# Attention features and a feed-forward on one core: block 0 turned by TensorE, two banks for small results, w1 scaled by halves, filled gaps, a new order

## The chip, the cores and the metric

The kernel runs on one core of a Trainium2 chip. TensorE (PE in the profile) multiplies matrices and writes to PSUM, eight banks of 512 fp32 columns; VectorE (DVE) and ScalarE (ACT) compute on tensors and read PSUM; GpSimd (POOL) computes on tensors in SBUF; SyncE (SP) issues the DMAs. Each engine works through its own instructions in order. The metric is device time of one execution in microseconds (us); 935.58 us is the median of three runs of the kernel before.

## The reference

Eight batches of eight heads, 576 positions, head size 64, 128 random features, then a feed-forward over the 4608 rows of 512:

```python
def phi(x):
    proj = einsum('bhsd,md->bhsm', x, omega)
    h = proj - sum(x * x, axis=-1, keepdims=True) / 2.0
    return exp(h - max(h, axis=-1, keepdims=True)) / sqrt(m)
q_p, k_p = phi(q * scale), phi(k * scale)
kv = einsum('bhsm,bhsd->bhmd', k_p, v)
z = sum(k_p, axis=2)
x = einsum('bhsm,bhmd->bhsd', q_p, kv) / (einsum('bhsm,bhm->bhs', q_p, z)[..., None] + 1e-06)
h = x.transpose(0, 2, 1, 3).reshape(4608, 512) @ w_in
out = maximum(0.01 * h, h) @ w_out
```

The weights `w_in` (512 x 2048) and `w_out` (2048 x 512) arrive as 64-bit floats, which the kernel converts on the chip.

## The kernel before

Most fp32 products are made of three fp16 products: each operand is scaled by a power of two and split into a high and a low half (`high` and `low_`, L358 and L373; the lines L369 and L375 of the profile are these two helpers).

The work is written as a list of operations with their engines, inputs, outputs and assumed durations. `Plan.order` (L128) puts them in one order before anything runs: it keeps a clock for each engine, places each operation at the earliest moment that its inputs, its buffer and its engine allow, and prefers those of lower `prio`. Products of the feed-forward are *fillers* with the last priority (`work = 1e6 + j`): they take PE whenever nothing else is ready. `PACE`, `LATER`, `NUDGE` and `SLACK` shift priorities and times. The result is a fixed order for each engine.

In order of the data:

- `omega` (L427) loads the feature matrix and scales and splits it.
- `key_batch(b)` (L786) makes `kv` of one batch. Batches 0 and 1 (`WHOLE = 2`) and query block 0 use class `Whole` (L665): the columns of k or q are loaded (L677), squared on ACT (L678), projected in full fp32 on PE (L699) into a bank pair `pj` or `pj0`; DVE takes the maximum (L706) and subtracts it (L708), ACT takes the exponential (L710). The sums over keys are L817. Later batches use class `Unit` (L560): fp16 halves, turned by a transposing DMA (L607), projected at L620.
- `values(b)` (L726) loads v (L739), finds its scale (L747 and `power_of_two`, L403) and, for batches 0 and 1, scales v in place (`high` at L762). `power_of_two` sends one column through PE into columns 384 to 511 of the bank `mi` (L409), then five small DVE operations follow.
- `query_block(j)` (L865) makes 512 rows of x. Block 0's features are turned by PE (L887) in fp32; the products with kv (L917) go to a bank `mi`, columns 0 to 259; DVE inverts and multiplies (L927 to L930) into `xp`. Then `parted` (L854) splits the rows into halves in a buffer `xn` and turns them by a transposing DMA (L862) into `xt`, whose columns are the tokens. There is one `xn` as long as `v1` lives.
- `Weight` (L457): eight 1 MB pieces of each matrix are loaded into four buffers `big` (L478, L480); ACT copies the high words (L493), DVE joins the low bits (L495, L498), PE sums magnitudes by column (L506, into a `ffn` bank `wsums` that is held until both matrices are through), the sign is put back by ACT and POOL (L511, L513) or DVE (L516). After all eight pieces `scale` (L519) finds one power of two for the matrix and `split` (L533) writes the halves (L540 or `high` and `low_`).
- `feed_forward(j)` (L1038): nine blocks of 512 rows. Blocks 0 and 1 make the first layer at L1059 (16 x 12 products of 512 columns), later blocks by a seven-product scheme at L1113; L1295 is the second layer, and L1220 that of the last two blocks. ACT applies the leaky maximum (L1068), and halves are split by ACT and POOL or DVE.

PSUM's eight banks: `pj` and `pj0` two each, three `ffn` and one `mi`; when the class `Whole` is through, the banks of `pj0` become two more for the feed-forward, called `late`.

Of the kernel before, what the change touches and what calls it, by code (L numbers as in the profile page):

```python
# [31 lines left out]
SPLIT_DVE = {"w1": [0, 1, 2, 4, 5, 7], "w2": [0, 1, 2, 3, 4, 5]}  # L32
Z_POOL = {"k": 6, "q": 7}
PACE = {"k": 17.0506, "q": 9.805, "w1": 0, "w1s": 2.5972, "w2": 15.4207, "w2s": 15.0}

WHOLE = 2
FIRST_FAST = 2
TAIL = 7
ROWS_LATE = 4
TAIL_ON = {"A11": ["DVE"], "A22": ["DVE"], "S1": ["DVE"], "S3": ["DVE"], "S2": ["POOL"], "A12": ["DVE"], "S4": ["DVE"], "T1": ["POOL"], "T2": ["DVE"], "T3": ["DVE"], "T4": ["DVE"]}  # L40
# [3 lines left out]
SLACK = {"PE": 0.5, "t": 0.5608, "qp": 0.5, "ph": 0.5, "mx": 0.5, "w": 0.25, "chain": 0.0804}  # L44
NUDGE = {"k00": -7.29, "w24": 1.48, "q61": -17.43, "k10": 0.44, "k51": 15.04, "q00": -3.82, "k53": 5.68, "w20": 3.7, "w2s6": 16.56, "k12": -4.82, "w1s0": 20.35, "q41": 14.5, "w1s4": -32.18, "w2s5": 11.73, "q72": -10.0, "q03": -2.3, "w1s7": 13.37, "w2s7": 35.19, "k61": -6.36, "w13": -2.71, "w2s3": -4.27, "q10": 5.76, "s1": -0.42, "k50": -35.27, "q70": 36.43, "q02": 2.72, "q40": 2.15, "k42": 7.0, "w25": 5.84, "q63": -12.37, "w27": 3.08, "k11": 0.9, "w26": 10.91, "w2s2": -8.29}
DMA = {"turn": 1.0, "land": 1.9}
SLOWER = {"ACT": 1.0, "DVE": 1.041, "POOL": 0.95, "PE": 1.0, "SP": 1.0}
EXP_ACT = {"k": [], "q": []}
XN_DVE = 0
SUMS_DVE = [2]  # L50
LATER = {"w1": -37.7982, "w2": 35.2434, "k": -22.3577, "q": -876.3298, "t": 0.05, "f": 0.0319, "s": -0.0535}
# [4 lines left out]
NUM_DOWN = 2.0 ** -12  # L56
OUT_UP = 2.0 ** 17 * 2.0 ** (-14 * 3)
# [5 lines left out]
PJ32 = 0.55  # L63

# [12 lines left out]
class Plan:  # L77
# [3 lines left out]
    HOP = {"PE": 0.25, "ACT": 0.08, "DVE": 0.08, "POOL": 0.10}  # L81
# [3 lines left out]
    def __init__(self, places):  # L85
        self.places, self.ops, self.over = places, [], {}
        self.wrote, self.read, self.kinds = {}, {}, {}
        self.now, self.nth, self.group = (None, 0.0), 0, None
# [10 lines left out]
    def op(self, ways, r=(), w=(), prio=0.0, slack=0.0, moved=0):  # L99
# [3 lines left out]
        o = Op()  # L103
        o.ways, o.prio, o.slack, o.moved = {e: way for e, *way in ways}, prio, slack, moved
# [23 lines left out]
    def order(self):  # L128
        free = dict.fromkeys(("PE", "ACT", "DVE", "POOL", "SP"), 0.0)
# [15 lines left out]
        for o in reversed(self.ops):  # L145
# [22 lines left out]
        def placed_at(o):  # L168
            t = o.ready
# [10 lines left out]
        while len(done) < len(self.ops):  # L180
# [86 lines left out]
def performer_ffn(ctx: ExitStack, tc, qT, kT, qn, kn, vn, omT, eye, w_in, w_out, out):  # L267
# [30 lines left out]
    banks = {"pj": (1, 1024), "pj0": (1, 1024), "ffn": (3, 512), "mi": (1, 512)}  # L298
# [88 lines left out]
    little, used_up = one("little", [P, 128]), [0]  # L387
# [39 lines left out]
    def omega():  # L427
        mx = small(1)
        op("SP", 0.45, lambda: nc.sync.dma_start(out=om32(), in_=omT), w=[(whole, "om")], moved=131072, prio=-0.9)
        op("SP", 0.45, lambda: nc.sync.dma_start(out=ident, in_=eye), w=["ident"], moved=65536, prio=-0.9)  # L430
# [23 lines left out]
        op("DVE", 1.3, split, r=[(whole, "om"), key], w=["om", "om_c"], prio=0.005)  # L454
# [943 lines left out]
```

## Time and profile before

| | us |
|---|---|
| median of three runs (931.43 to 936.42) | 935.58 |
| the profiled execution | 934.21 |
| its span, first to last instruction | 932.4 |
| PE busy in it | 886.1 |
| DVE busy | 751.1 |
| ACT busy | 608.9 |
| POOL busy | 326.6 |
| mean granted clock of PE | 0.979 of full |

Busy time of PE is not useful time alone: at a lower granted clock the same products are busy for longer. A wait in the tables is put down to the instruction that came last. The idle time of an engine matters only where that engine is on the way to the end.

### The profile page before, as it was taken

The numbers are of one execution on the slowest core, as the hardware profiler recorded it, in microseconds if no ns is written. First come the engines' busy times: TensorE is split into PE (matmuls) and PEld (weight loads), VectorE is DVE, ScalarE is ACT, GpSimd is POOL, SyncE is SP. The second block draws the span as 40 slices with busy tenths as digits, with TensorE's granted clock in tenths as the row PEclk, the third lists the DMA queues.
The fourth block names the chain that finished last, engine by engine and source line by source line (L and its number), as shares of the span: only waits on it lengthen the run. The fifth ranks groups of instructions, "written<-read, shape, count | busy, mean of one in ns | idle before, by whom it ended". The sixth has DMA issues, their size and how long they took to land.

```text
span 932.4 us, 20377 instructions
## 1 busy us (share of the span) xinstructions
PE 886.1 (95%) x8102; PEld 636.3 (68%) x8102; DVE 751.1 (81%) x1384; ACT 608.9 (65%) x905; POOL 326.6 (35%) x290
## 2 busy tenths in 40 slices
PE   4796999999999799999999999999999999999998
PEld 3784466555554686578658955786579657888887
DVE  7889888888889698888778987977988788993861
ACT  4777796557765687479756874796568555753741
POOL 2243446657765344117212531162115222210010
PEclk8698899999999999999999999999999999999999
DMA  9779234967479998689789997888598876633401
GB/s 365 288 206 298 62 58 104 239 169 152 108 151 278 278 261 195 174 219 257 171 184 230 247 223 183 210 235 186 111 234 219 199 158 164 177 75 94 134 1 46
DMA packets 279103, 171.17 MB, mean 184 GB/s; under 512 B 195296, under 2 KB 242144, under 8 KB 277984
## 3 DMA queue, kind: packets, MB, share of 16 engines
q1 hardware_dynamic: 279008, 169.87, 72.2%
q8 instruction: 63, 1.03, 0.5%
q14 instruction: 32, 0.26, 0.1%
HBM read 105.87 MB, written 16.78 MB: 132 GB/s over the span
## 4 chain that ended last, share of the span: by engine, by line
PE 79%; DVE 11%; DMA 5%; issue 1%; ACT 1%; SPq 1%; DVEq 0%; ACTq 0%
PE ffn L1295 15%; PE ffn L1113 15%; PE late L1295 11%; PE late L1113 10%; PE ffn L1059 5%; PE pj L620 5%; PE ffn L1220 5%; PE late L1220 3%; PE pj L699 2%; PE mi L817 2%; DMA qp<-ph 1%; DMA t<-z 1%; DMA xt<-xn 1%; DVE wt L498 1%; PE mi L910 1%
## 5 line engine op out<-in xcount | busy, mean ns | idle before, releaser
L1113 PEld LDWEIGHTS <-w 128*128 128x128 f16 x2352 | 227.4, 98 | 36.8 <-issue 6.8
L375 POOL TENSOR_TENSOR big<-row,big 128x512 f16<-128x512 f32 x116 | 150.2, 1306 | 258.9 <-ACT big L369 249.4
L1295 PEld LDWEIGHTS <-big 128*128 128x128 f16 x1344 | 127.2, 98 | 136.4
L1295 PE MATMUL ffn<-wt,big 128*128 128x512 f16 x816 | 190.2, 379 | 0.0
L1113 PE MATMUL ffn<-xt,w 128*128 128x256 f16 x1044 | 139.5, 273 | 3.3 <-DMA xt<-xn 3.3
L1295 PE MATMUL late<-wt,big 128*128 128x512 f16 x528 | 124.1, 379 | 0.0
L651 ACT ACTIVATE p<-p,little 128x1024 f32<-128x1024 f32 x68 | 70.1, 1030 | 55.5 <-DVE p L648 55.4
L628 DVE TENSOR_REDUCE st<-pj 128x8 f32<-128x1024 f32 x68 | 73.1, 1074 | 27.8 <-PE pj L620 27.4
L1113 PE MATMUL late<-xt,w 128*128 128x256 f16 x660 | 92.8, 273 | 0.0
L1059 PE MATMUL ffn<-xt,w 128*128 128x512 f16 x312 | 73.9, 388 | 8.5 <-DMA xt<-xn 8.2
L369 ACT ACTIVATE big<-row 128x512 f16<-128x512 f32 x128 | 77.2, 622 | 2.9 <-DVE row L1085 2.4
L648 DVE SCALAR_TENSOR_TENSOR p<-pj,sc,st 128x1024 f32<-128x1024 f32 x68 | 77.0, 1133 | 0.7
L375 DVE TENSOR_TENSOR ph<-p,ph 128x1024 f16<-128x1024 f32 x56 | 72.7, 1297 | 4.9 <-ACT ph L369 4.7
L580 ACT ACTIVATE z<-nat 128x512 f32<-128x512 f32 (+1 forms) x56 | 36.3, 649 | 57.6 <-DMA t<-z 46.8
L1059 PEld LDWEIGHTS <-w 128*128 128x128 f16 x384 | 37.0, 99 | 51.0 <-issue 12.3
L620 PE MATMUL pj<-om,t 128*128 128x128 f16 x944 | 63.8, 219 | 3.0 <-DMA t<-z 2.4
L620 PEld LDWEIGHTS <-t 128*128 128x128 f16 x944 | 57.5, 98 | 13.2 <-DMA t<-z 3.7
L1113 PE MATMUL ffn<-w,w 128*128 128x256 f16 x360 | 58.9, 273 | 1.7 <-ACT z L1240 1.7
L369 ACT ACTIVATE ph<-p 128x1024 f16<-128x1024 f32 x56 | 58.8, 1050 | 0.7
L375 POOL TENSOR_TENSOR v<-xp,v 128x768 f16<-128x768 f32 (+1 forms) x15 | 26.2, 1745 | 89.0 <-ACT v L369 88.9
L582 DVE TENSOR_REDUCE sq<-z 128x8 f32<-128x512 f32 (+1 forms) x56 | 39.5, 706 | 18.2 <-ACT z L580 18.1
L1136 ACT ACTIVATE row<-row 128x512 f32<-128x512 f32 x71 | 43.8, 624 | 11.3 <-DVE row L1129 11.1
(236 smaller groups left out, 1809.8 us busy)
## 6 DMA issues: line engine op xcount, KB each, us to landing
w<-w1d SPq DMA_DIRECT2D x196, 256.0 KB, 3.3
v<-vn SPq DMA_DIRECT2D x28, 650.0 KB, 4.7
big<-w_in SPq DMA_DIRECT2D x8, 1024.0 KB, 10.2
big<-w_out SPq DMA_DIRECT2D x8, 1024.0 KB, 5.7
nat<-qn SPq DMA_DIRECT2D x32, 256.0 KB, 3.9
out<-row SPq DMA_DIRECT2D x32, 256.0 KB, 2.6
w1d<-wt SPq DMA_DIRECT2D x16, 256.0 KB, 3.3
nat<-kn SPq DMA_DIRECT2D x12, 320.0 KB, 3.5
```

Source lines behind the costliest of these rows:

```text
L369: ("ACT", act(n, int(pointer)), lambda: nc.scalar.activation(dst(), src(), AF.Copy, scale=1.0 if scale is None else value()), False),
L375: return ways([(e, c, lambda g=g: g.tensor_tensor(dst(), a(), b(), op=ALU.subtract), True) for e, c, g in (("POOL", pool_(n), nc.gpsimd), ...
L582: op("DVE", dve(n), lambda: nc.vector.tensor_reduce(at(self.sq)[:, :2 * nt], square().rearrange("p (g d) -> p g d", d=D), axis=AX.X, op=AL ...
L620: nc.tensor.matmul(at(pj)[:, 512 * h + c * M:512 * h + (c + 1) * M], at(self.t)[:, 2 * (c0 + c) + h, :], om[:, w, :], start=(w == 0), stop ...
L628: op("DVE", dve(n * M), lambda: nc.vector.tensor_reduce(row(0), pv(), axis=AX.X, op=ALU.max), r=[pj], w=[st], prio=prio)
L648: op("DVE", dve(n * M), lambda: nc.vector.scalar_tensor_tensor(p(), pv(), down(), row(2).rearrange("p (g o) -> p g o", o=1).broadcast_to([ ...
L651: op("ACT", act(n * M, 1), lambda: nc.scalar.activation(flat(p()), flat(p()), AF.Exp, bias=shift), w=[p32], r=["ones"], prio=prio)
L1059: nc.tensor.matmul(at(ph), wk[wp][:, c:c + P], xt[:, 512 * xp:512 * xp + 512], start=(i == 0), stop=(i == 3 * KT - 1))
L1113: nc.tensor.matmul(pair(bank)[:, f], wt[:, k, wp, f * P:f * P + P], operand(xname, k, xp), start=(first and f == k == i == 0), stop=(k == ...
L1136: op("ACT", act(512), lambda: nc.scalar.activation(at(g), at(src), AF.Prelu, scale=H_DOWN * (TAIL_DOWN if tail else 1.0), alpha=0.01), r=[ ...
L1220: nc.tensor.matmul(pair(bank)[:, t], g()[:, gp, f, t * P:t * P + P], operand(wname, 2 * q + f, wp), start=(first and q == t == f == i == 0 ...
L1295: nc.tensor.matmul(at(po), g_(q)[:, s, gp, t * P:(t + 1) * P], wf[wp], start=(q == s == 0 and gp == wp), stop=(q == s == 3 and gp == 1))
```

## The change

- `TURNED = 1`: block 0's rows are turned by PE transposes into an `ffn` bank, and the halves are made from there by ACT and DVE (`turned_parts`); `parted` with its DMA is not used for it.
- `FFN_MI = [2, 2]`: two fixed `ffn` banks instead of three, two `mi` banks instead of one. The weights' column sums lie in unused columns of `mi` 0.
- w1 gets one scale for pieces 0 to 3 and one for 4 to 7; the first half can be split when four pieces are converted. w2's scale takes both into account. w2's sums add pairs of columns.
- `HEAT`: where the planned order leaves PE a gap of over 0.3 us ahead of the first filler, products that nobody reads (240 columns, into `mi` 1) are put in.
- Batches 0 and 1: v is not scaled; its column of ones is divided instead, and the scale goes into the eviction of kv. The exponentials of `Whole` lose their shift.
- `LOW_ACT`: for one piece of w1 and three of w2 ACT shifts the low word, and one DVE operation joins instead of two. `EDGE_ACT`: one edge's exponential is taken straight from PSUM by ACT. `SQ_POOL`: two squares by POOL.
- `Whole` has buffers of its own kinds, four `raw` and three `sqz`, that lie over `nat`, `t`, `xn`, `z` and `p32`; batch 1's operations are listed ahead of query block 1's.
- The planner's figures (`HOP`, `LESS`, `SLOWER`, `SLACK`, `PACE`, `LATER`, `NUDGE`, issue costs) change, and it now models the clock of PE. A second, backward pass exists but is not run (`PASSES = 0`). `EXP_ACT`, `Z_POOL`, `SPLIT_DVE` and `TAIL_ON` move some later operations between engines.

```diff
-SPLIT_DVE = {"w1": [0, 1, 2, 4, 5, 7], "w2": [0, 1, 2, 3, 4, 5]}
-Z_POOL = {"k": 6, "q": 7}
+SPLIT_DVE = {"w1": [0, 1, 2, 4, 5, 7], "w2": [0, 1, 2, 3, 4, 5, 6]}
+Z_POOL = {"k": 6, "q": 6}
+TURNED = 1
+HEAT = True
+PASSES = 0
+EDGE_ACT = ['k02']
+SQ_POOL = ['k02', 'k13']
+LOW_ACT = {"w1": [3], "w2": [1, 4, 5]}
+FFN_MI = [2, 2]
...
-SLOWER = {"ACT": 1.0, "DVE": 1.041, "POOL": 0.95, "PE": 1.0, "SP": 1.0}
-EXP_ACT = {"k": [], "q": []}
+SLOWER = {"ACT": 1.0223, "DVE": 1.0399, "POOL": 0.95, "PE": 1.0, "SP": 1.0}
+EXP_ACT = {"k": [], "q": [1]}
...
-    HOP = {"PE": 0.25, "ACT": 0.08, "DVE": 0.08, "POOL": 0.10}
+    HOP = {"PE": 0.25, "ACT": 0.13, "DVE": 0.12, "POOL": 0.13}
+    LESS = {"PE": 0.0, "ACT": 0.08, "DVE": 0.08, "POOL": 0.08, "SP": 0.0}
...
+                if HEAT and not o.filler and not begun and t - s > 0.3:
+                    x = Op()
+                    n = int((t - s - 0.1) / (0.2 if cold else 0.1))
...
+                    x.run, x.prio, x.filler, x.heat = (lambda n=n: self.warm[1](n)), 1e7, True, True
...
+                begun = begun or o.filler
...
-    banks = {"pj": (1, 1024), "pj0": (1, 1024), "ffn": (3, 512), "mi": (1, 512)}
+    banks = {"pj": (1, 1024), "pj0": (1, 1024), "ffn": (FFN_MI[0], 512), "mi": (FFN_MI[1], 512)}
...
+    for k, hosts in (("raw", (("nat", 0), ("nat", 1), ("t", 0), ("xn", 0))), ("sqz", (("z", 0), ("z", 1), ("p32", 0)))):
+        for host in hosts:
+            over[host] = [(k, len(tiles[k]))]
...
+        def heat(n):
+            for _ in range(n):
+                nc.tensor.matmul(tiles["mi"][1][:, 4 * E:4 * E + 240], om[:, 0, :],
+                                 om.rearrange("p a b -> p (a b)")[:, :240], start=True, stop=True)
+        plan.warm = done, heat
...
-            self.sums, self.col0 = wsums, 64 * (name == "w2")
+            first = 4 * E + 64 * (name == "w2")
+            self.sums = tiles["mi"][0][:, first:first + (32 if name == "w2" else 64)]
...
+            if i in LOW_ACT[self.name]:
+                op("ACT", act(1150), lambda: nc.scalar.activation(shifted(), low(), AF.Copy, scale=LOW_DOWN, bias=LOW_LESS),
+                   r=[b], w=[tmp], prio=prio)
+                op("DVE", stt(1024), lambda: nc.vector.scalar_tensor_tensor(shifted(), bits(), 3, shifted(),
+                   op0=ALU.logical_shift_left, op1=ALU.bitwise_or), port=True, r=[f], w=[tmp], prio=prio)
...
+            if self.name == "w1":
+                mxs, key = small(8), f"w1{half}"
...
+                op("DVE", 0.4, run, r=[("sums", "w1", 4 * half + i) for i in range(4)], w=[f"mx_{key}"], prio=prio)
+                self.pow[half], self.key[half] = power_of_two(mx, key, prio, ONE / 4)
+                return
...
-                x = lambda dst=dst: dst()[:, :, :D]
-                high(half * D, x, x, lambda: t[:, 0:1], r=[key], w=[k], prio=prio)
+                op("DVE", 0.2, lambda dst=dst: nc.vector.tensor_scalar(dst()[:, :, D:], dst()[:, :, D:], t[:, 1:2], 1.0 / ONE,
+                   op0=ALU.mult, op1=ALU.mult), r=[key], w=[k], prio=prio)
...
+    def turned_parts(xt, at_, src, keys, prio):
+        bank = buf("ffn")
+        part = lambda i: at(xt).rearrange("p i c d -> p (i c d)")[:, 1024 * at_ + 512 * i:1024 * at_ + 512 * i + 512]
+        def turn():
+            x = src().rearrange("p a b -> p (a b)")
+            for c in range(4):
+                nc.tensor.transpose(at(bank)[:, c * P:(c + 1) * P], x[:, c * P:(c + 1) * P], ident)
+        op("PE", 4 * 0.12, turn, r=[*keys, "ident"], w=[bank], prio=prio)
+        high(512, lambda: part(0), lambda: at(bank), psum=True, r=[bank], w=[(xt, at_, 0)], prio=prio)
+        op("DVE", stt(512), lambda: nc.vector.tensor_tensor(part(1), at(bank), part(0), op=ALU.subtract),
+           r=[bank, (xt, at_, 0)], w=[(xt, at_)], prio=prio)
...
-    wsums = buf("ffn")
...
-    for w in (w1, w2):
-        for i in range(8):
+    for w, some, half in ((w1, range(4), 0), (w1, range(4, 8), 1), (w2, range(8), 0)):
+        for i in some:
...
                 parts.append(key_batch(done_k, 0.0))
+                if done_k < WHOLE:
+                    in_turn(parts.pop())
```

More of the change, by code (lines that the diff above doesn't have):

```diff
@@ L128, in order, with backward, latest, forward @@
     def order(self):
+        done = self.forward()
+        for _ in range(PASSES):
+            late = self.backward(done)
+            for o in self.ops:
+                if not o.filler and o.prio > -0.9:
+                    o.prio = -0.5 + 1e-4 * (late[o.number] + SHIFT_OP.get(o.number, 0.0))
+            done = self.forward()
+        return done
+    def backward(self, done):
+        held, at_ = {}, {}
+        done = [o for o in done if not o.heat]
+        for o in done:
+            o.needs = {x.number: x for x in o.before}
+            for b in o.bufs:
+                if b not in at_:
+                    hosts = [(b.kind, b.place), *self.over.get((b.kind, b.place), ())]
+                    at_[b] = [held[k] for k in hosts if k in held]
+                    held[b.kind, b.place] = b
+                for x in (x for u in at_[b] for x in u.ops):
+                    o.needs[x.number] = x
+            o.needs.pop(o.number, None)
+        left = dict.fromkeys((o.number for o in done), 0)
+        for o in done:
+            for x in o.needs:
+                left[x] += 1
+        last = max(o.end for o in done)
+        until, late = dict.fromkeys(left, last), {}
+        free = dict.fromkeys(("PE", "ACT", "DVE", "POOL", "SP"), last)
+        port = last
+        todo = [o for o in done if not left[o.number]]
+        while todo:
+            cost = lambda o: o.cost - self.LESS[o.engine]
+            def latest(o):
+                r = min(until[o.number] - (o.end - o.start - cost(o)), free[o.engine])
+                return min(r, port) if o.held else r
+            o = max(todo, key=lambda o: (latest(o), o.start))
+            start = latest(o) - cost(o)
+            todo.remove(o)
+            late[o.number] = free[o.engine] = start
+            if o.held:
+                port = start
+            for n, x in o.needs.items():
+                until[n] = min(until[n], start)
+                left[n] -= 1
+                if not left[n]:
+                    todo.append(x)
+        return late
+    def forward(self):
+        for bs in self.kinds.values():
+            for b in bs:
+                b.place = b.last = None
+        busy, window, cold, begun, heaters = {}, 0, True, False, 0
+        for o in self.ops:
+            o.start, o.heat = None, False
         free = dict.fromkeys(("PE", "ACT", "DVE", "POOL", "SP"), 0.0)
@@ L788, in key_batch @@
         plan.group = f"v{b}"
+        plan.after = AFTER["k1"] if b == 1 else 0.0
         values(b, prio)
@@ L795, in key_batch @@
             plan.like("k", PACE["k"])
+            plan.after = AFTER["k1"] if b == 1 else 0.0
             plan.group = f"k{b}{hp}"
@@ L868, in query_block @@
             plan.like("q", PACE["q"])
+            plan.after = AFTER["q1"] if j == 1 else 0.0
             plan.group = f"q{j}{hp}"
@@ L1039, in feed_forward @@
         plan.like()
+        plan.after = 0.0
         plan.group = None
```

217 lines of the change are left out of this document (146 added, 71 removed).

## The prediction

> **What bounds the kernel now.** I read the page first: its span and the rows of busy tenths.
>
> ```profile
> span 932.4 us, 20377 instructions
> PE   4796999999999799999999999999999999999998
> DVE  7889888888889698888778987977988788993861
> PEclk8698899999999999999999999999999999999999
> ```
>
> TensorE (PE) is full in nearly every slice except the first four, about 93 us, where it is also granted a low clock. So PE sets the pace from there to the end, and in the opening something else does. The table of windows says how much is lost where (columns: window, length, then busy time and instructions of PE, weight loads, DVE, ACT, POOL, then granted clock, DMA share, GB/s).
>
> ```profile
> 0.00:20.00 20.00, 9.96 (x90) 8.75 (x92) 13.67 (x27) 11.65 (x12) 6.03 (x6) 0.83 0.90 356
> 20.00:40.00 20.00, 12.33 (x134) 11.63 (x131) 18.53 (x25) 13.24 (x15) 6.33 (x8) 0.75 0.87 353
> 40.00:60.00 20.00, 17.96 (x182) 17.27 (x181) 15.50 (x29) 12.02 (x16) 5.82 (x3) 0.76 0.54 181
> 60.00:80.00 20.00, 17.92 (x178) 15.29 (x178) 17.66 (x29) 19.92 (x27) 6.48 (x3) 0.98 0.97 253
> 80.00:100.00 20.00, 11.81 (x104) 7.02 (x101) 19.93 (x23) 11.23 (x15) 7.05 (x6) 0.74 0.85 225
> 100.00:200.00 100.00, 99.54 (x745) 57.19 (x744) 85.34 (x157) 70.03 (x96) 54.33 (x54) 1.00 0.56 125
> 200.00:400.00 200.00, 191.82 (x1681) 119.92 (x1680) 167.04 (x316) 132.85 (x195) 101.29 (x102) 1.00 0.81 200
> 400.00:800.00 400.00, 398.55 (x3860) 286.65 (x3858) 333.19 (x660) 275.20 (x417) 127.98 (x103) 1.00 0.84 201
> 800.00:933.00 133.00, 126.24 (x1152) 112.60 (x1151) 80.27 (x124) 62.78 (x116) 11.33 (x9) 0.99 0.29 81
> ```
>
> PE idles 10.0 + 7.7 + 2.0 + 2.1 + 8.2 = 30.0 us in the first 100 us, 0.5 in the next 100, 8.2 from 200 to 400, 1.4 from 400 to 800. After 100 us there is little left to win. In the opening DVE is the fullest engine: 18.5 of 20 us, then 15.5, 17.7, 19.9. The waits of PE in the first 110 us name what it stood for:
>
> ```profile
> PE ffn L506 <- DVE wt L498: 8.4, 4, 4.2
> PE ffn L1059 <- DMA xt<-xn: 8.2, 2, 4.9
> ...
> PE mi L409 <- DVE xp L930: 1.2, 1, 1.2
> ...
> PE pj L699 <- DMA nat<-kT: 1.1, 2, 0.5
> ```
>
> The first line is PE waiting on a busy DVE and costs nothing by itself. The second is the path: the first product of the feed-forward (L1059) waits for block 0's turned rows. The timeline shows how the last quarter of them arrives:
>
> ```profile
> 84.38 0.42 DVE L930 TENSOR_TENSOR xp<-mi,r 128x256 f32<-128x256 f32 x1
> 88.12 1.44 PE L1059 MATMUL ffn<-xt,w 128*128 128x512 f16 x3 [3.25 <-DMA xt<-xn]
> 88.19 0.63 ACT L369 ACTIVATE xn<-xp 128x512 f16<-128x512 f32 x1 [4.26 <-DVE ph L708]
> 88.89 2.05 POOL L375 TENSOR_TENSOR xn<-xp,xn 128x512 f16<-128x512 f32 x1 [1.95 <-ACT xn L369]
> 90.97 1.26 SPq L862 DMA_TRANSPOSE xt<-xn  x1
> 94.48 5.26 PE L1059 MATMUL ffn<-xt,w 128*128 128x512 f16 x15 [4.91 <-DMA xt<-xn]
> 102.57 6.63 PE L1059 MATMUL ffn<-xt,w 128*128 128x512 f16 x30
> ```
>
> The rows are ready at 84.80 and reach PE at 94.48, 9.7 us later: ACT starts the halves only at 88.19, just when the transfer before it has landed (88.12), there being one `xn`; then POOL, then the transfer. From 94.48 on PE is full, so each us by which that start moves is a us of the end, if later stages keep up.
>
> **The change, part by part.** Times are set against the profiled execution: 934.21 us, of which 932.4 are span and 1.8 lie around it; the median shown, 935.58, is 1.4 above it.
>
> 1. Block 0 turned by PE (TURNED, `turned_parts`). Four transposes per pair of heads, then the halves by ACT and DVE out of PSUM; the four xn transfers with their issues on SP, the ACT copies and the POOL subtractions of block 0 go. The prices:
>
> ```profile
> 71.98 1.09 PE L887 MATMUL ffn<-ident,ph 128*128 128x128 f32 x8
> L369 ACT ACTIVATE qp<-ffn 128x512 f32<-128x512 f32 x8 | 4.4, 585 | 0.7 <-PE ffn L887 0.7
> L1129 DVE TENSOR_TENSOR row<-ffn,row 128x512 f32<-128x512 f32 x6 | 4.1, 685 | 0.9 <-ACT z L1136 0.6 <-ACT row L369 0.4
> ```
>
> Eight transposes take 1.09, so four take 0.55; with 0.59 on ACT, 0.69 on DVE and about 0.4 of hand-overs (an estimate; gaps between engines in the rows above are 0.1 to 0.2) the quarter is ready 2.2 us after its rows instead of 9.7: 7.5 gained, the PE wait of 8.2 being the limit. The other three subtractions come from POOL to DVE, which is full here: 3 x 0.69 = 2.1 lost. The 16 transposes, 2.2 on PE, lie in its idle time. Net **5.4** (3 to 8).
>
> 2. Unread products in gaps (HEAT) and v left unscaled. In the opening the same work takes two prices:
>
> ```profile
> 36.26 7.79 PE mi L817 x40
> 48.54 1.23 DVE L706 TENSOR_REDUCE st<-pj 128x8 f32<-128x1024 f32 x1 [3.94 <-PE pj L699]
> 155.77 2.23 PE mi L817 x20
> L369 ACT ACTIVATE v<-v,little 128x1280 f32<-128x1280 f32 x2 | 2.7, 1356 | 0.5 <-DVE little L418 0.5
> ```
>
> Forty of the key sums took 7.79 cold against 2 x 2.23 = 4.46 warm; behind them DVE stood 3.94 us. The warm clock gives back 3.3, and the two ACT scalings of 1.36 that stood before the sums go (four small DVE operations on the ones columns come; between the 0.15 and the 0.28 of the rows in part 3, I take 0.2), so this wait vanishes: **3.9** (0 to 3.9). At the start of the feed-forward 15 products took 5.26 against 6.63 / 2 = 3.3 warm: **2.0** (0 to 2.8) if no gap lies ahead of it, since the plan inserts no heating once a product is placed. Heating products stand in PE's queue, so what PE executes behind them (projections, sums, then DVE's maxima) comes later where a gap was planned too long. Lower end 0, other end the idle of 20 to 60 us, 9.7, if lateness can no longer be absorbed there; I take 0, as one such product (240 columns, so about 0.1 by 6.63 / 30 for 512) is the size of a hand-over.
>
> [...]
>
> 3. Weight scales by halves. One more scale, priced by the scale of v:
>
> ```profile
> 31.64 0.28 DVE L413 TENSOR_REDUCE little<-mi 128x1 f32<-128x128 f32 x1
> 32.53 0.15 DVE L418 TENSOR_SCALAR little<-little 128x1 f32<-128x1 f32 x1
> ```
>
> From 31.64 to 32.68 is 1.04 on DVE. In return the splits of w1's first half no longer wait for the eighth piece; they were not last (the wait above is for xt), but after part 1 they would be near it. LOW_ACT takes one L495 of w1 (0.84, below) from DVE, and three of w2 later, for a pass of ACT each, which is busy only 13.2 and 12.0 of 20 us from 20 to 60; the edge of k02 leaves DVE with one 128x256 operation (0.42, as L930); the ones columns cost 0.8. Sum before the start: -1.04 + 0.84 + 0.42 - 0.8 = **-0.6** (-2 to +1).
>
> 4. Buffers and order. Four raw buffers remove the 1.1 of `nat<-kT`: **1.0** (0 to 1.1). They lie over `nat`, `t` and `xn`, so query block 1's loads into `nat` are now held behind batch 1's last projection, and behind them on SP its transfers; block 1's products wait for these, a whole block (some 80 us of PE) later, so I price it at 0 and count a longer delay under part 7. The new order can put off what the first products do not need:
>
> ```profile
> L498 DVE SCALAR_TENSOR_TENSOR wt<-big,wt 128x1024 uint32<-128x1024 uint32 x14 | 17.8, 1282 | 0.0
> L706 DVE TENSOR_REDUCE st<-pj 128x8 f32<-128x1024 f32 x10 | 12.1, 1218 | 7.4 <-PE pj L699 7.4
> L495 DVE TENSOR_SCALAR wt<-wt 128x1024 uint32<-128x1024 uint32 x14 | 11.8, 840 | 0.8 <-ACT wt L493 0.8
> ...
> L747 DVE TENSOR_REDUCE little<-v 128x1 f32<-128x1280 f32 x4 | 5.9, 1475 | 0.0
> ```
>
> Up to 95 us DVE converted 14 pieces where 8 are w1, did ten maxima where 8 belong to batch and block 0, and both reductions of v1: 6 x 2.12 + 2 x 1.22 + 2 x 1.48 = 18 us early. But the second layer needs all of w2 by its start, so I take a fifth, **4** (0 to 9). HOP, LESS, SLOWER and SLACK issue nothing; they only choose the order.
>
> 5. Two mi banks, ffn from three plus two late to two plus two. The bank of the sums returns to none: in the opening two stayed usable before too. Later one is missing; a bank's eviction (0.59) is covered by the 2.6 us of 12 products on the next, so **0** (-3 to +1).
>
> 6. EXP_ACT, Z_POOL, TAIL_ON move work between engines that are not the bound after 100 us: **0** (-2 to +2).
>
> 7. Given back. Block 2 starts in a hole of its own:
>
> ```profile
> 290.00:300.00 10.00, 7.87 (x75) 4.36 (x73) 8.74 (x17) 6.75 (x9) 5.91 (x7) 1.00 0.92 269
> 300.00:310.00 10.00, 7.95 (x76) 5.33 (x75) 8.97 (x22) 5.63 (x9) 4.60 (x3) 1.00 1.02 215
> 310.00:320.00 10.00, 8.78 (x89) 7.95 (x89) 4.45 (x7) 4.49 (x7) 2.76 (x6) 1.00 1.07 299
> ```
>
> PE loses 5.4 us here, with DVE at 87 and 90% in the first two rows and the DMA engines full: supply is last. If PE comes earlier, supply must too. I take **-3** (-13 to +5).
>
> Sum: 5.4 + 3.9 + 2.0 - 0.6 + 1.0 + 4 + 0 + 0 - 3 = 12.7 gained. 934.2 - 12.7 = 921.5 for a profiled execution; plus 1.4 for the median: **923**.
>
> **The rivals.**
> - *Given back at block 2.* The opening gains 15.7, the hole at 290 to 320 grows by 13. For: DVE is at 84% between 100 and 400 and fuller just before the hole. Against: the keys and queries of blocks 1 and 2 also start earlier. Then 2.7 are left: 933, no change that a measurement of this kernel can tell (about 0.5%, 4.7 us).
> - *Waits in the shared mi banks (slower).* The sums of the weights move from a bank of their own into mi 0, heating goes to mi 1. The wait of L409 on L930 above, 1.2 us, is between columns 384 on and columns 0 to 259 of one bank: no overlap, still a wait. If each of the 16 sums stands 1.2 for a read queued on the full DVE, PE stands 19.2, with the projections behind it: 12.7 - 19.2 = 6.5 slower, 942. It decides from 11 of the 16 on (12.7 / 1.2). Against: a second mi bank halves the meetings, and the planner can place sums late. [...]
> - *Order does far more.* DVE puts off 9 instead of 4, nothing is given back and the hole at 290 closes: 12.7 + 5 + 3 + 5.4 = 26 gained: 909. For: the 18 us of early work; against: the second layer's need of w2.
>
> **How the numbers follow.** Forecast 0.66, given back 0.16, shared banks 0.12, far more 0.06. Faster by over 0.5%: 0.66 + 0.06 and a little of the second, 0.74; within: 0.14; slower: 0.12. The range leaves out the slower rival and the far end, 0.18: 910 to 934.
>
> **What would show it.** Right: no L862 for block 0, first full row of L1059 at 80 to 85 instead of 94.48; PE clock near 1.00 from 20 us to there; the L817 run near 4.5 us; DVE's wait of 3.94 gone. Wrong: waits of PE on mi readers of several us, new waits on ffn banks after 150, PE busy in 280 to 320 under 80%. The forecast fails if w1's first half, not xt, is late at 85, or if the new order opens holes after 100 us, where PE now loses 17 in all.

## The result, and the profile after

The change makes the kernel **slower: 948.0 us** (median of 4 runs, 945.22 to 948.23) against 933.5 us of the kernel before in the same comparison (4 runs, 930.85 to 936.42), a ratio of 1.0148 with a 95% interval of 1.0106 to 1.019. The forecast was 923 us, the range 910 to 934. The page of the kernel after (span, busy tenths, the chain of waits by engine and by line):

```profile
span 946.1 us, 20741 instructions
PE   7998899999998899999999999999999999999998
PEclk9998999999999999999999999999999999999999
PE 52%; DVE 26%; DMA 9%; ACT 7%; issue 3%; SPq 1%; POOL 1%; DVEq 0%; ACTq 0%; POOLq 0%
L763 PE MATMUL pj<-om,t 128*128 128x128 f16 x944 | 64.5, 220 | 15.3 <-DVE p L791 6.8
```

In the opening PE is busier (86.4 of the first 100 us instead of 70.0, though 17.0 of them are unread products) and warmer (a granted clock of 0.97 instead of 0.81), as the table below shows. But slices 13 and 14 now have eights, and the chain that ended last runs through PE for only 52% of the span. In the page of before that line was:

```profile
PE 79%; DVE 11%; DMA 5%; issue 1%; ACT 1%; SPq 1%; DVEq 0%; ACTq 0%
```

The table of windows tells where PE now loses (columns as in the prediction; after first, then before in the same cuts):

```profile
0.00:100.00 100.00, 86.43 (x912) 71.99 (x913) 87.72 (x149) 71.53 (x89) 32.70 (x23) 0.97 0.74 263
100.00:200.00 100.00, 94.85 (x714) 53.68 (x713) 89.04 (x174) 68.80 (x101) 50.74 (x58) 1.00 0.67 152
200.00:500.00 300.00, 281.43 (x2561) 183.79 (x2560) 249.93 (x481) 209.89 (x331) 132.31 (x124) 0.99 0.83 195
500.00:925.00 425.00, 421.13 (x3919) 319.69 (x3918) 313.87 (x581) 263.85 (x431) 125.90 (x93) 1.00 0.66 162
```

```profile
0.00:100.00 100.00, 69.98 (x670) 59.96 (x671) 85.29 (x131) 68.06 (x82) 31.70 (x24) 0.81 0.83 273
200.00:500.00 300.00, 291.82 (x2653) 191.31 (x2652) 248.11 (x483) 206.08 (x307) 130.88 (x124) 1.00 0.82 202
500.00:925.00 425.00, 421.51 (x4012) 325.17 (x4012) 331.52 (x613) 264.75 (x423) 109.73 (x90) 1.00 0.68 165
```

From 100 to 200 us PE idles 5.2 us instead of 0.5, from 200 to 500 18.6 instead of 8.2; after 500 the two are alike. That is 15 us more of idle time, and the clock of 0.99 from 200 to 500 takes about 3 us more (1% of 281). DVE and DMA are somewhat fuller than before from 100 to 200 us (89.0 instead of 85.3 us, 0.67 instead of 0.56); from 200 to 500 DVE and ACT do 1 and 2% more. The waits of PE between 200 and 500 us, after and then before:

```profile
PE pj L763 <- DVE p L791: 6.1, 6, 2.0
PE pj L763 <- DMA t<-z: 4.9, 3, 2.9
PE mi L1087 <- DMA qp<-ph: 2.7, 1, 2.7
PE mi L1089 <- DMA qp<-ph: 1.1, 3, 0.6
...
```

```profile
PE ffn L1113 <- DMA xt<-xn: 3.3, 1, 3.3
PE mi L912 <- DMA qp<-ph: 2.1, 1, 2.1
PE pj L620 <- DMA t<-z: 2.1, 1, 2.1
PE pj L620 <- DVE p L648: 0.6, 1, 0.6
```

Before has four waits in 300 us; after has thirteen in these rows alone, all at the projections (L763) and numerators (L1087, L1089) of later blocks. In six of them the projection waits for DVE (L791), which still reads the bank pair `pj`. Two of the rows that are left out here are waits for a feed-forward bank, 0.7 us each; none is for a reader of `mi`.

To see when the lead was won and lost, the products that the result needs can be counted along each record, every kind at one warm price (18 products of 512 columns in 3.88 us, for instance; unread products at nothing), and the count of before taken off at the same time. Worked out in that way from the traces, the lead over the record of before in us:

```
at us                       100   180   260   300   340   500   700   900
after                       9.2   3.9  -0.3  -3.3  -4.5 -12.2 -14.9 -13.7
no_heat_same_order          5.1  -1.0  -6.2  -8.3 -10.6 -19.7 -22.3 -20.9
held_turned                 5.5   0.0   0.5  -0.6  -3.1  -3.7  -5.7  -7.2
held_heat                   4.4   4.7   5.2   4.6   1.7   1.1  -1.7  -1.9
held_both                   4.9   4.5   5.0   3.4   1.0   0.7   0.0  -1.2
held_both_swap              6.8   0.7   1.3   2.2   1.4   0.1  -0.9  -1.9
held_both_loads_later       4.6   3.5   4.2   4.2   2.6   2.5   1.3   0.0
held_both_less_dma          4.6   4.1   4.8   4.2   8.0   7.6   6.4   4.8
held_swap                   3.6   3.0   3.3   3.0   1.4   1.4   1.1   1.1
held_loads_later            1.3   0.9   1.4   2.3   2.0   2.0   1.4  -0.5
held_less_dma               1.9   1.5   2.2   2.3   4.8   4.7   4.5   3.1
held_less_pe, plus 6.9      (*)   4.5   5.0   5.4   0.8   0.0  -3.2  -4.8
```

(*) 2.9 without the 6.9 us that it leaves out between 100 and 180 us. The last four rows have the opening of before, instruction for instruction, and still lie 1.3 to 3.6 us ahead of its record at 100 us: records of one order differ by that much there. So the opening of the kernel after has won about 7 us (9.2 less their mean of 2.4), not 15.7, and the lead is gone by 260 us. From 100 to 700 us it loses 24 us against the record of before (9.2 to -14.9).

### The profile page after: what moved, and what is told of

It is laid out like the page before. It is cut to its first block, busy times and chain, and to the rows that moved or that the text cites. A ratio compares the mean times of both kernels' runs of the same rounds, so it can differ in the third digit from the quotient of the medians.

```text
span 946.1 us, 20741 instructions
## 1 busy us (share of the span) xinstructions
PE 900.9 (95%) x8256; PEld 644.2 (68%) x8256; DVE 744.1 (79%) x1390; ACT 615.6 (65%) x955; POOL 341.7 (36%) x296
## 4 chain that ended last, share of the span: by engine, by line
PE 52%; DVE 26%; DMA 9%; ACT 7%; issue 3%; SPq 1%; POOL 1%; DVEq 0%; ACTq 0%; POOLq 0%
PE ffn L1481 10%; PE late L1481 9%; PE ffn L1299 8%; PE late L1299 8%; PE late L1406 6%; PE pj L763 4%; DMA t<-z 3%; DVE ph L486 3%; PE ffn L1406 2%; DMA big<-w_in 2%; DVE st L771 2%; DVE p L791 2%; PE late L1245 2%; DMA qp<-ph 1%; DVE z L486 1%
## 5 line engine op out<-in xcount | busy, mean ns | idle before, releaser
L486 POOL TENSOR_TENSOR big<-row,big 128x512 f16<-128x512 f32 x113 | 152.9, 1362 | 217.0 <-ACT big L480 198.4
L1481 PE MATMUL ffn<-wt,big 128*128 128x512 f16 x672 | 160.6, 381 | 0.0
L1481 PE MATMUL late<-wt,big 128*128 128x512 f16 x672 | 159.1, 379 | 0.0
L1299 PE MATMUL late<-xt,w 128*128 128x256 f16 x864 | 116.7, 273 | 1.8 <-ACT row L480 1.1
L1299 PE MATMUL ffn<-xt,w 128*128 128x256 f16 x840 | 115.2, 273 | 1.6 <-ACT row L480 1.6
L794 ACT ACTIVATE p<-p,little 128x1024 f32<-128x1024 f32 (+1 forms) x60 | 61.2, 1020 | 57.9 <-DVE p L791 57.8
L763 PE MATMUL pj<-om,t 128*128 128x128 f16 x944 | 64.5, 220 | 15.3 <-DVE p L791 6.8
L763 PEld LDWEIGHTS <-t 128*128 128x128 f16 x944 | 58.0, 98 | 28.5 <-issue 10.5
L486 POOL TENSOR_TENSOR xn<-xp,xn 128x768 f16<-128x768 f32 (+1 forms) x16 | 28.3, 1770 | 110.9 <-ACT xn L480 82.8
L791 DVE SCALAR_TENSOR_TENSOR p<-pj,sc,st 128x1024 f32<-128x1024 f32 (+1 forms) x60 | 67.1, 1118 | 0.7
L1245 PE MATMUL ffn<-xt,w 128*128 128x512 f16 x264 | 60.7, 379 | 1.3 <-ACT row L1254 1.2
L1299 PE MATMUL ffn<-w,w 128*128 128x256 f16 x336 | 55.0, 273 | 0.0
```

The lines of the kernel that those rows point to most:

```text
L486: return ways([(e, c, lambda g=g: g.tensor_tensor(dst(), a(), b(), op=ALU.subtract), True) for e, c, g in (("POOL", pool_(n), nc.gpsimd), ...
L763: nc.tensor.matmul(at(pj)[:, 512 * h + c * M:512 * h + (c + 1) * M], at(self.t)[:, 2 * (c0 + c) + h, :], om[:, w, :], start=(w == 0), stop ...
L791: op("DVE", dve(n * M), lambda: nc.vector.scalar_tensor_tensor(p(), pv(), down(), row(2).rearrange("p (g o) -> p g o", o=1).broadcast_to([ ...
L794: op("ACT", act(n * M, 1), lambda: nc.scalar.activation(flat(p()), flat(p()), AF.Exp, bias=shift), w=[p32], r=["ones"], prio=prio)
L1245: nc.tensor.matmul(at(ph), wk[wp][:, c:c + P], xt[:, 512 * xp:512 * xp + 512], start=(i == 0), stop=(i == 3 * KT - 1))
L1299: nc.tensor.matmul(pair(bank)[:, f], wt[:, k, wp, f * P:f * P + P], operand(xname, k, xp), start=(first and f == k == i == 0), stop=(k == ...
```

## The experiments

Two theories at first: **the order** (the plan's new figures choose an order that is worse after 100 us, whatever the new parts gain) and **the parts** (some moved or added piece costs time where it stands). Where no interval is given, a run is one execution.

### Which part of the change costs the time

The unread products are left out at their places in the order:

```diff
-            for _ in range(n):
+            for _ in range(0):
                 nc.tensor.matmul(tiles["mi"][1][:, 4 * E:4 * E + 240], om[:, 0, :],
```

> The changed kernel in its own order, with the 136 unread products left out and nothing else changed. If they do what they are for, the opening is cold again: key sums and projections at twice the price, the first product of the feed-forward later than 85.1 us by 3 to 6, the whole 3 to 5 us slower (950 to 953). If instead they hold PE up (they wait for readers of their bank), it is 1 to 4 us faster. In both cases the holes of PE between 220 and 500 us stay (28 us lost there against 8).

Measured 955.01 us, beside 934.88 for before. The unread products are worth about 7 us (955.01 - 948.0, the first a single execution), a little more than was expected here and than the forecast gave them together with the unscaled v (3.9 + 2.0). They are no cause of the loss.

The tables that move later work between engines as before (`EXP_ACT`, `Z_POOL`, `SPLIT_DVE`, `TAIL_ON`), and in another kernel `NUDGE`, `PACE` and `LATER` as before:

```diff
-EXP_ACT = {"k": [], "q": [1]}
+EXP_ACT = {"k": [], "q": []}
...
```

> The changed kernel with EXP_ACT, Z_POOL, SPLIT_DVE and TAIL_ON as before, so that the eight query units have their exponential in one ACT pass after DVE again. Theory 'moved work' (the eight 0.47 us passes per unit hold the only pj pair and delay the chain): the lead of the opening is kept, 928 to 935, and PE's waits for DVE p fall from 6.8 us to under 1. Theory 'order without cushion': 940 to 950, with as much PE idle after 200 us.

> The changed kernel with NUDGE, PACE and LATER of before. If the new order was spoiled by these shifts: 928 to 938. If figures or moved work are the cause: 943 to 953, with the holes between 220 and 500 us at other places but of the same sum.

Measured 956.70 and 955.87, more than either theory expected. Both are slower than the kernel after, but each of them also gives another order, so by its time alone neither run can clear its group of edits. The waits of after_old_engines say more: with the exponentials moved back, PE still waits 8.3 us at its projections for DVE to finish with `pj`, where 'moved work' wanted under 1 (6.8 in the kernel after):

```profile
L763 PE MATMUL pj<-om,t 128*128 128x128 f16 x944 | 64.7, 221 | 14.4 <-DVE p L791 8.3
```

The next run changes the order alone: the kernel before, with only the plan's figures of the change. No operation differs, and each engine has as many instructions as before; only the order differs, and with it the places of the buffers.

```diff
-    HOP = {"PE": 0.25, "ACT": 0.08, "DVE": 0.08, "POOL": 0.10}
+    HOP = {"PE": 0.25, "ACT": 0.13, "DVE": 0.12, "POOL": 0.13}
+    LESS = {"PE": 0.0, "ACT": 0.08, "DVE": 0.08, "POOL": 0.08, "SP": 0.0}
...
```

> The kernel before with only the planner's figures changed (HOP, LESS, SLOWER, SLACK, DMA and the issue costs): no instruction differs, only the order. Theory 'order without cushion': 8 to 18 us slower than before (942 to 952), PE idle after 200 us up from 17 to 25 or more. Theory 'moved work' or 'banks': within 3 us of before.

Measured **957.99**: 23 us from the order alone, with the instructions of before. Measured against this order the whole change *gains* 10 us (957.99 to 948.0). It also has the kinds of wait of the kernel after, with the instructions of before (waits of PE from 100 to 925 us; before has 0.6 us of the first kind and 2.6 of the second, the kernel after 6.8 and 4.7):

```profile
PE pj L621 <- DVE p L649: 7.0, 5, 2.8
PE mi L913 <- DMA qp<-ph: 5.5, 7, 1.3
```

### Are the new figures special, or any other order?

The same instructions in four more orders: one priority moved by 5 (`"w1s0": 20.35` to `15.35`), one factor of the plan by 1% (POOL 0.95 to 0.96), the new durations alone, the new `SLACK` alone.

> Control: the kernel before with one shift of its order changed (NUDGE of w1s0 from 20.35 to 15.35); no instruction and no figure of a duration differs, the order differs from the first sixth of the operations on. Theory 'figures' (short durations and no slack spoil the order): within 8 us of before, 928 to 943. Theory 'chosen order' (the order of before is one of many and was kept because it ran well; any other costs the same as a new figure): 945 to 960.

> Second control: the kernel before with SLOWER of POOL 0.96 instead of 0.95, which changes the order from the first fifth on. 'Figures': 928 to 943. 'Chosen order': 945 to 960.

> The kernel before with the new durations alone (HOP, LESS, SLOWER, DMA, issue costs; SLACK as before). 'Figures', if it is the durations: 950 to 960, like all figures together (958.0). If it is the slack: 930 to 943.

> The kernel before with the new SLACK alone (qp, mx and chain at 0, ph 0.69). If the slack is the cause: 945 to 958. If the durations are: 930 to 943.

Measured 963.59, 945.12, 955.59 and 952.97, beside 935.53. The theory that the figures are at fault falls: edits without any meaning cost as much. With before_new_figures, five other orders of the same instructions lie 10 to 28 us above before. The order of before is the fastest of the six. Nor do the holes have one place. PE's idle time, from the windows of each:

| us | 100–200 | 200–500 | 500–925 |
|---|---|---|---|
| before | 0.5 | 8.2 | 3.5 |
| after | 5.2 | 18.6 | 3.9 |
| before_new_figures | 6.5 | 12.3 | 6.2 |
| before_other_order_1 | 1.2 | 13.7 | 17.0 |
| before_other_order_2 | 0.7 | 9.7 | 11.5 |

### The parts on an order that is held

If the order is the cause, the new parts should gain on the order of before. It is written out as a list (number of the operation, engine, buffer places), and `Plan.order` returns it:

```diff
+HELD = "2D0 0S0 1S 17S0 143S0 150S1 157S2 3D0 164S3 ..."
...
+        for word in HELD.split():
...
+            o = by_number.pop(n)
+            o.run = o.ways[engines[letter]][1]
```

held_turned turns the second half of block 0 by PE, with three operations moved behind it; held_heat puts 184 unread products into the gaps of the opening; held_both does both, with 109.

> The kernel before in its own order, which is written out and held, with one part of the change: the second half of block 0's rows (pairs of heads 2 and 3) is turned by PE into an ffn bank and split by ACT and DVE. Three moves in the order make room: one early half product, the sums of one weight piece and one square of ACT go behind the first products that use these rows. Theory 'the part works, the new order spoils it': first full row of L1059 at 87 to 89 us instead of 94.5, the lead kept to the end, 4 to 6 us faster (928 to 931 where before is 934). Theory 'the parts are worth nothing': within 2 us of before.

> The kernel before in its own held order with the unread products alone (184 of 240 columns, into the unused columns of the bank of the weight sums, in the places where PE stood). 'The part works': granted clock near 1.00 from 15 us on, key sums 4.5 us instead of 7.8, the first products after 94.5 us warm (3.3 instead of 5.3 us for 15), 2 to 5 us faster. 'Worth nothing' or filled gaps that hold PE up: within 2 us, or slower.

> Both parts on the held order (109 unread products, none at the feed-forward's start). 'The parts work': the sum of the two less what they share, 6 to 9 us faster than before (925 to 928), and faster than the changed kernel by 20. 'Worth nothing': within 2 us of before.

| | us | ratio to before (95%) |
|---|---|---|
| held_turned | 941.24 | 1.0056 [1.0033, 1.008] |
| held_heat | 936.29 | 1.002 [0.9993, 1.0046] |
| held_both | 935.70 | 1.0008 [0.9991, 1.0025] |

So the parts gain nothing even there, and held_turned alone is slower, clear of the noise: its record loses its lead between 100 and 180 us, where PE waits 2.3 us for the scale of w2 (L620) and 0.8 for ACT to empty a feed-forward bank (L1290), and its clock is 0.98; before has none of this there. The table of leads says more. The four records with held_both's opening are 4.6 to 6.8 us ahead at 100 us, against 1.3 to 3.6 of the four with the opening of before, so the two parts win some 3 us there. held_heat and held_both keep a lead of 5 us until 260 us and have 1 to 2 left at 340. That is where the first rival of the prediction, given back at block 2, put the loss. The waits of PE from 285 to 345 us of held_both:

```profile
PE mi L1137 <- DMA qp<-ph: 3.2, 1, 3.2
PE pj L831 <- DMA t<-z: 2.3, 1, 2.3
PE mi L1135 <- DMA qp<-ph: 1.4, 1, 1.4
...
```

With 0.4 us for `xt` they are 7.3 us in all. But before waits as long in the same stretch: 7.5 us, the three waits of 3.3, 2.1 and 2.1 that are shown above. What differs between the two records is the granted clock (held_both, then before):

```profile
285.00:345.00 60.00, 52.69 (x504) 41.50 (x503) 44.52 (x87) 38.45 (x61) 22.69 (x24) 0.91 0.96 250
285.00:345.00 60.00, 52.47 (x529) 40.61 (x528) 49.31 (x95) 38.89 (x62) 27.62 (x26) 1.00 1.02 276
```

At 0.91 the 52.7 busy us do 4.7 us less work than at full clock, and the lead falls by 4.0 from 260 to 340 us. held_heat has 0.94 here and loses 3.5, held_both_loads_later (below) 0.97 and loses 1.6. So in these records the hole did not grow with the lead; the lower clock around its waits took the lead. The clock is not all of it, though: the mean clock of held_both's ten executions goes from 0.985 to 0.992, and their times do not follow it (935.24 us at 0.985, 935.06 at 0.992). What takes the time where the clock falls less is not on record.

### What takes the lead at the start of block 2

Four theories: PE stands in its fixed order in front of a product that is not ready while others are (held_both_swap, with held_swap as its control); the supply of the next block is late whatever PE does (held_less_pe); the DMA engines are full (held_both_less_dma); the place of the loads on SP's queue (held_both_loads_later).

```diff
-... 1237T0,0 782T2,2,1 783T2,8,1 784T3,0,1 ... 1246T0,1,0,0 ... 1055T5,2,0,3 ... 1064T7,1,3,2
+... 782T2,2,1 783T2,8,1 1237T0,0 784T3,0,1 ... 1055T5,2,0,3 1064T7,1,3,2 1246T0,1,0,0 ...
```

> Both opening parts on the held order as in held_both (935.70), and four groups of feed-forward products (5.2 us of PE work) moved ahead of the two products that wait at the start of block 2 (2.34 us for t at 290 us; 1.39 and 3.15 us for qp at 316 us). Theory 'given back at block 2 because PE stands behind a wait in its fixed order': the waits shrink to about 1.5 us in all, the clock of 290 to 345 comes back to 1.00 and the lead of 5 us survives: 927 to 931. Rival 'the other engines' supply sets the end, whatever stands in front of the wait': the waits come back at the next product that needs their rows, 934 to 937.

> The order of before with the same four groups moved, without the opening parts: the control of held_both_swap. Before waits 2.13 us for t and 2.1 us for qp at these places. Theory 'fixed order': about 3 us faster than before, 931 to 933, and held_both_swap lies 2 to 5 us below it. Rival 'supply sets the end': 934 to 936, and the two agree.

Measured 934.08 (0.9997 [0.9972, 1.0023]) and 933.15 (0.9994 [0.9971, 1.0018]). The two waits did shrink, to 1.2 us on `qp` and none on `t`, and others came in their place:

```profile
PE mi L620 <- DVE little L960: 2.2, 1, 2.2
PE mi L1137 <- DMA qp<-ph: 1.2, 1, 1.2
...
```

The first of these is for the scale of a v; all of them are 5.0 us. The control does as well without any of the opening parts. In the record of held_both_swap, though, the lead was already lost between 100 and 180 us, so this pair alone does not settle what happens at 290.

In held_less_pe a third of half of block 0's first layer is not computed, 6.9 us of PE:

```diff
                         for wp, xp in ((0, 0), (0, 1), (1, 0)):
+                            if j == 0 and f >= 8 and wp:
+                                i += 1
+                                continue
```

> The order of before; 32 products of block 0's first layer (rows times the low part of the weights, output tiles 8 to 15) are left out, 32 x 0.2158 = 6.9 us of PE work between 100 and 150 us, nothing else. Theory 'given back at block 2': PE arrives there 6.9 us earlier and waits longer, most of the 6.9 us is lost there: 932 to 935, with the lead gone by 345 us. Rival 'the sum of PE's work sets the end': 927 to 929.

Measured **939.05, slower** than before by 0.63% [0.35, 0.91], and above what either theory expected. It is the clearest of the runs: 6.9 us less for an engine that is busy 95% of the span, and the time goes up by 4.8. From 100 to 180 us (held_less_pe, then before) 4.6 of the 6.9 become idle time, the longest waits (1.5 and 1.2 us) for results of DVE:

```profile
100.00:180.00 80.00, 75.31 (x610) 45.17 (x609) 69.44 (x121) 59.47 (x84) 46.31 (x46) 1.00 0.56 121
```

```profile
100.00:180.00 80.00, 79.95 (x614) 47.08 (x612) 68.02 (x118) 58.30 (x81) 44.86 (x41) 1.00 0.51 107
```

The rest is gone by 345 us: from 285 on PE waits 8.2 us (3.1 and 2.0 for `qp` and 1.9 for `xt` among them) against 7.5, and its clock there is 0.94 instead of 1.00, worth 3 us of its 51.8 busy ones. From 345 to 925 us it idles 3.8 us more than before. So a full row of PE did not mean that the other engines had time to spare.

In held_both_less_dma 20 of block 2's weight loads are not issued:

```diff
-            o.run = o.ways[engines[letter]][1]
+            o.run = (lambda: None) if n in UNSENT else o.ways[engines[letter]][1]
```

> held_both without 20 loads of 256 KB of first-layer weights of block 2 (the tiles keep what they held before), so DMA carries 5 MB less between about 280 and 360 us, where its busy share is 0.86 to 1.03. Theory 'DMA is full at the start of block 2, and that makes t and qp late': the waits for t and qp shrink by more than half, 928 to 932. Rival 'VectorE and ScalarE make these rows late': the waits stay at about 6.9 us, 934 to 937.

> The control of held_both_less_dma: the order of before without the same 20 loads of 256 KB of block 2's first-layer weights (the tiles keep what they held before), and without the opening parts. Theory 'with the transfers light enough the opening's lead survives': between before and held_both_less_dma's 929.5, 931 to 933. Rival 'the missing loads alone give the 5 us, the lead of the opening counts for nothing': 928 to 930.

Measured 929.5 for the one and 933.7 for its control (0.9985 [0.9966, 1.0003]; its profiled execution took 931.05). The first is a single execution, below all 20 of before in its comparison (929.85 to 938.53). Its lead grows over the start of block 2, from 4.2 to 8.0 us (its control's from 2.3 to 4.8). PE is busy there for 56.1 of 60 us at full clock, in held_both for 52.7 at 0.91 (above):

```profile
285.00:345.00 60.00, 56.13 (x604) 45.35 (x603) 51.24 (x104) 44.88 (x71) 27.96 (x28) 1.00 0.78 189
```

By the two profiled executions the opening's part in the gain is 1.6 us, by the control's median 4.2; one execution is too little to say which. The trace shows what the loads do. SP's queue in held_both, then without the loads (start, length, operation):

```profile
304.17 2.85 SPq L1334 DMA_DIRECT2D w<-w1d  x6
...
310.11 2.76 SPq L818 DMA_TRANSPOSE t<-z  x1
...
313.60 1.38 SPq L1103 DMA_TRANSPOSE qp<-ph  x1
```

```profile
304.77 1.11 SPq L1236 DMA_DIRECT2D w1d<-wt  x2
307.61 2.00 SPq L821 DMA_TRANSPOSE t<-z  x1
309.71 2.63 SPq L1106 DMA_TRANSPOSE qp<-ph  x2
```

With the loads in front, SP issues `t` 2.5 and `qp` 3.9 us later. So the last pair leaves all loads in and issues twelve of them behind these transfers:

```diff
-... 1056S6 1063S7 1066S1 ... 1071S2 ... 1291S0,0 1077S3 1244S0,0 1083S8 1086S9 1245S0,0 1088S10
+... 1056S6 ... 1291S0,0 1244S0,0 1245S0,0 1063S7 1066S1 1071S2 1077S3 1083S8 1086S9 1088S10
```

> held_both (935.70) with twelve loads of first-layer weights issued later on SP's queue and nothing else moved: six behind the transfer of t that is issued at 284.6 us, six behind the two transfers of qp that are issued at 313.6 and 316.2 us. Theory 'at the start of block 2 the rows of the next query block stand behind weight loads on SP's queue' (six loads hold it from 304.2 to 307.0 us, and the kernel without 20 loads issues t and qp 2.5 and 3.9 us earlier): the waits for t and qp there fall from 6.9 to below 2.5 us, and the lead of the opening survives: 929 to 932. Rival 'the transfers themselves are too many, wherever they are issued': the waits come back as waits for w, 934 to 937.

> The order of before with the same twelve loads issued later, without the opening parts: the control of held_both_loads_later. Theory 'SP's queue': also faster than before, by 1 to 4 us (930 to 933), and held_both_loads_later lies 1 to 4 us below it, because only there PE has a lead to keep. Rival 'too many transfers': 934 to 937. If the two agree, the lead of the opening is worth nothing even then.

Measured 933.75 (0.9999 [0.9987, 1.001]) and 933.63 (0.9994 [0.9977, 1.0011]). The waits for `t` are gone and those for `qp` down to 1.2 us, as this theory wanted; but PE waits 7.0 us there all the same: 2.3 us for `xt`, 1.8 for the scale of a v and 1.4 for ACT to empty a feed-forward bank have come in their place. So the place of the loads on the queue sets *which* row is late. That their amount sets how late the rows are in all fits the run without the loads; it is not shown, since the medians have not confirmed it and 3.2 of the 7.0 us are waits for DVE and ACT.

Of the kernels with all their work, none is faster than before; the best medians, 933.15 to 934.08, cannot be told from it.

## Why the prediction was wrong

**The step that failed is part 4.** It said of the plan's figures that they "issue nothing; they only choose the order", took 4 us of gain in the opening for the new order and nothing behind it. In its place the runs showed that the order alone cost 23 us in before_new_figures, with the kinds of wait of the kernel after, and 10 to 28 us in the four other orders of the same instructions. The prediction named the sign itself ("if the new order opens holes after 100 us") and gave it no price. It had read 99.5% busy from 100 to 200 us and 99.6% from 400 to 800 as a kernel bound by PE, with little left to win or lose behind the opening. The runs fit another reading of those rows: the work of four engines and one DMA queue meets closely in one order, and a different order, less work for PE (held_less_pe) or an earlier start does not meet it.

**Part 7, given back, was mis-sized.** It took 3 us, with 13 as one end. On the held order all but 1 to 2 of 5 us are gone at 340 us. That is where the prediction put the loss, but not how: the waits there are no longer than before's, and the clock is lower. In the kernel after the lead is lost before that, in many waits of 1 to 3 us from 110 to 500. The rival of that name forecast a hole grown by 13 us, which none of these records shows, and ended at 933, since it too left the order out.

**Part 2 did most of what it said, part 1 only a part.** The first products start early, and the 40 key sums are warm (start, length, operation; the first and the last group of the sums, then the rows up to the first products and one behind them):

```profile
38.51 1.11 PE L976 MATMUL mi<-v,ph 128*128 128x65 f32 x8 [0.60 <-DVE v L918]
...
43.04 0.39 PE L976 MATMUL mi<-v,edge 128*128 128x65 f32 x2
...
75.73 1.11 PE L1094 MATMUL mi<-kv,qp 128*128 128x65 f32 x8 [2.47 <-ACT qp L480]
...
77.06 1.19 DVE L865 TENSOR_TENSOR ph<-pj,st 128x1024 f32<-128x1024 f32 x1
...
78.45 0.73 DVE L1107 TENSOR_TENSOR xp<-mi,r 128x256 f32<-128x256 f32 x2
...
79.23 1.76 PE L570 MATMUL mi<-om 128*128 128x240 f16 x8 [1.91 <-DVE xp L1107]
...
80.92 0.80 PE L847 MATMUL pj<-xt,t 64*128 64x128 f32 x4
...
82.36 0.64 PE L847 MATMUL pj<-xt,z 64*128 64x128 f32 x4
...
84.62 0.66 PE L1035 MATMUL ffn<-ident,xp 128*128 128x128 f32 x4
85.12 2.75 PE L1245 MATMUL ffn<-xt,w 128*128 128x512 f16 x12
...
85.95 0.69 DVE L1038 TENSOR_TENSOR xt<-ffn,xt 128x512 f16<-128x512 f32 x1 [2.71 <-ACT xt L480]
...
90.92 0.39 PE L847 MATMUL pj<-xt,p 64*128 64x128 f32 x4
```

The sums take 4.9 us with it (forecast 4.46, before 7.79); DVE's wait of 3.94 us is gone (2.1 in all are left on `pj`); the first row of the feed-forward starts at 85.12, at the end of the 80 to 85 that the prediction set, and its 12 products take 2.75, warm.

Part 1 allowed 2.2 us from the rows of the last quarter to its halves. Here the rows are ready at 79.18 us (78.45 + 0.73) and the last half at 86.64 (85.95 + 0.69), 7.5 us later: in PE's fixed order 8 unread products and 32 projections stand between the rows and their turning at 84.62. From the last rows to the first full row of products it is 5.9 us (79.18 to 85.12) instead of 9.7, so about 4 us are won there and not 7.5.

The clock is 1.00 from 0 to 60 us. It fell to half once in the rest of the opening, around the waits of 2.47 and 1.91 us (0.87 in the us from 77, 0.50 from 78 to 84, 0.72 in the us from 84, 1.00 from 85): the projections at 82.36 took 0.64 where the same took 0.39 at 90.92. The 2.0 us of the first products were kept, but these projections stand ahead of them. The unread products did not prevent it, and here they held PE up: by the row at 79.23 they waited 1.91 us themselves, for DVE to finish reading an `mi` bank, and the projections behind them started at 80.92, 2.67 us after DVE was done with `pj` at 78.25 (77.06 + 1.19). Without unread products, in no_heat_same_order, the same projections follow DVE by 0.06 us:

```profile
83.74 1.19 DVE L865 TENSOR_TENSOR ph<-pj,st 128x1024 f32<-128x1024 f32 x1
...
84.99 0.80 PE L847 MATMUL pj<-xt,t 64*128 64x128 f32 x4 [0.76 <-DVE ph L865]
```

The prediction named such lateness in part 2 and took 0 for it; at this place it is 2.6 us. Three of the four turnings by PE came before the waits of 2.47 and 1.91 us, and the last one, 0.66 us at 84.62, as the full clock came back. What turning by itself does to the clock is not shown.

**Parts 3, 5 and 6.** Part 5 stayed within its range: waits for feed-forward banks are 1.4 us from 200 to 500 us, where before has none. The rival with shared `mi` banks came only in small: the unread products waited twice for a reader of `mi`, 2.4 us in all, where 16 waits of 1.2 were feared. Part 3 was not tried by itself. Part 6 cannot be parted from the order: after_old_engines moved both.

**Open:** the parts gain about 10 us against before_new_figures and none against before. Each is one comparison of orders that differ, so what the parts are worth by themselves cannot be told more closely. Two `ffn` banks, the scale of w1 by halves, `LOW_ACT` and the buffers of `Whole` did not run on a held order. So that the order, and none of these, takes the time in the kernel after is argued from the other orders and from its waits; no run shows it alone.

## What to carry to other kernels

- When an edit lets a planner choose a new static order, the new order is an edit with its own price. Move one priority or one factor that means nothing, run it, and take the spread that comes (here 10 to 28 us) as what the order can do; to judge a part by itself, hold the order as a list.
- Before counting an earlier start as an earlier end, look at the next hole behind it, and ask which queue supplies it and what PE's clock does around it. Leaving out some of the work that is thought to be the bound, as in held_less_pe, tells whether it is.
- A row of nines on one engine shows that it is busy, not that the others have slack: in held_less_pe 6.9 us less work for PE came with 4.8 us more in all.

## What the runs showed of the hardware

- Behind a short wait PE's clock was 0.50. In held_swap the wait took 1.94 us, up to 298.89 us (windows of 1 us; the clock is the third figure from the end):

```profile
297.00:298.00 1.00, 0.00 (x0) 0.00 (x0) 1.00 (x2) 0.51 (x1) 1.00 (x1) 1.00 1.08 210
298.00:299.00 1.00, 0.10 (x1) 0.11 (x1) 0.97 (x3) 0.00 (x0) 1.00 (x2) 1.00 0.90 166
299.00:300.00 1.00, 1.00 (x4) 0.51 (x5) 1.00 (x1) 0.63 (x1) 0.12 (x1) 0.58 1.13 213
300.00:301.00 1.00, 1.00 (x4) 0.33 (x3) 0.97 (x4) 0.00 (x0) 0.00 (x0) 0.50 1.25 136
301.00:302.00 1.00, 1.00 (x4) 0.43 (x3) 0.73 (x2) 0.00 (x0) 0.00 (x0) 0.50 0.63 146
302.00:303.00 1.00, 1.00 (x9) 0.79 (x7) 0.21 (x2) 0.69 (x1) 0.00 (x0) 0.71 0.98 255
```

  Full clock (1.00) is back in the window from 303 us, so by an estimate from the clocks of four windows the wait costs 1.7 us more than it lasts (0.42 + 0.50 + 0.50 + 0.29). The record of before has one of 3.3 us, up to 311.22, with a granted clock of 1.00 in all windows from 300 to 320, so length alone does not decide.
- Issuing takes time: on SP's queue in held_both six loads held it for 2.85 us and the two transfers that turn `qp`'s rows for 1.38 and 1.24. Those rows waited for the queue, and the queue not for them: their transfers, at 313.60 and 316.17, follow the loads ahead of them by 0.10 and 0.09 us (312.97 + 0.53 and 315.07 + 1.01), and among SP's own waits from 280 to 330 us none is at L1103.
